# Four widths for each expert's matmuls, chosen on TensorE by the expert's token count

## The chip, the cores and the metric

The program runs on one core of one Trainium2 chip. The metric is device time in microseconds of one execution; before the change it is 400.27 us, the median of three runs (399.86 to 400.37). Engines are named as in the profile: PE is TensorE's matmul, PEld its weight load, PEldq its sequencer, DVE is VectorE, ACT ScalarE, POOL GpSimd, SP SyncE.

## What is computed

A retention layer (a decaying linear attention) is followed by a mixture of experts with one expert for each token:

```python
# q, k, v: (4, 8, 768, 64); x below has N = 3072 rows of D = 512
state = gamma * state + outer(k[t], v[t]);  y[t] = scale * q[t] @ state
...
logits = x @ w_gate                       # E = 8 experts
expert_idx = argmax(logits, axis=1);  gate_w = softmax(logits)[expert_idx]
for e in range(E):
    xe = x[expert_idx == e]
    h = maximum(xe @ w1[e], 0.0)          # 512 -> 1024
    out[expert_idx == e] = gate_w * (h @ w2[e])   # 1024 -> 512
```

How many tokens an expert gets is known only when the gate has been computed.

## The kernel before

The first 126 us compute the retention in chunks of 128 positions, the gate, and a scatter of the rows of x to one region of DRAM for each expert. Expert 0 is taken in two halves of up to 224 tokens: the first beside the last attention work, the second as step `e == 0` of `moe_main`. The other seven experts are sorted on the chip by their counts, the largest first, and take steps `e` = 1 to 7. Step `e` has a fixed room of `CAPS[e]` tokens (452, 424, 412, 400, 392, 376, 360), and its matmuls always work on all of it, however many tokens came. Tokens beyond the room would be left to `moe_rest`, behind a branch at the end (L646).

`moe_main` writes its order out by hand (`manual_schedule`). In a step, PE does eight *first-layer groups* (`f` = 0 to 7, L850): twelve matmuls each, three products of split operands (high by high, low weights by high, high weights by low) over four slices of D, into a PSUM tile `ph` of 128 features by `cap` tokens. ACT makes `hh` from `ph` (a ReLU, L855) and DVE `hl` (the rest that rounding leaves, L856). Then come four *second-layer groups* (`k` = 0 to 3, L878) of 24 matmuls each into `py`, 128 by `cap` again; DVE turns `py` into rows (L797). In steps 0 and 7 the second layer is done the other way round, tokens on the output's partitions and 512 columns wide (L876); there `cap` sets only how many partitions are used. `ph` is a ring of three PSUM tiles: group `f` can start when `hl` of group `f - 3` is done.

Around these groups the list `jobs` places other work behind the group where it stands: the loads of the next expert's weights (SP, L129), their split in high and low parts (ACT L137, DVE L138), the next expert's rows (`prep_x`), and the scatter of the last expert's results (POOL, L659).

Of the kernel before, what the change touches and what calls it, by code (L numbers as in the profile page):

```python
# [9 lines left out]
F32 = mybir.dt.float32  # L10
F32R = mybir.dt.float32r
BF16 = mybir.dt.bfloat16
I32 = mybir.dt.int32
AF = mybir.ActivationFunctionType
ALU = mybir.AluOpType
AX = mybir.AxisListType

B, H, S, D = 4, 8, 768, 64
E, DM, F = 8, 512, 1024
N = B * S  # L20
P = 128
# [5 lines left out]
NTOK = N // P  # L27
CAPS = [224, 452, 424, 412, 400, 392, 376, 360]
EARLY = 224
CMAX = max(CAPS)  # L30
CMAX32 = -(-CMAX // 32) * 32
E1 = E - 1
E9 = E + 1
KD = DM // P
KF = F // P
# [4 lines left out]
JMAX = -(-CMAX // 32)  # L40
# [17 lines left out]
_n = 0  # L58
for _name, _w in (("causal", 128), ("cv", 6 * H), ("ratio", 6 * (H // 2)), ("ident", 128), ("iota", 8),
                  ("desc", 16), ("tok", NTOK), ("blk", 24), ("ebase", E9),  # L60
                  ("rev", E1), ("eid", E1), ("caps", E1), ("row", 4), ("gate", 4 * E), ("slot", JMAX), ("place", 4)):
    OFF[_name] = (_n, _n + _w)
    _n += _w
NCONST = _n
# [3 lines left out]
def _constants():  # L68
    p = np.arange(P)
    c = np.zeros((P, NCONST), np.float64)  # L70

    def put(name, v):
        a, b = OFF[name]
        c[:, a:b] = v

    gamma = 1.0 - 2.0 ** (-5.0 - np.arange(H, dtype=np.float64))
    put("ident", np.eye(P))
    put("causal", (p[None, :] >= p[:, None]).astype(np.float64))
    put("iota", np.broadcast_to(np.arange(8)[None, :], (P, 8)))
    pos = (np.arange(6)[None, :] * C + p[:, None] + 1).astype(np.float64)  # L80
    put("cv", (gamma[None, None, :] ** (-pos[:, :, None])).reshape(P, 6 * H))
    order = np.concatenate([np.arange(E), np.arange(1, E), [0]])
    put("desc", np.broadcast_to(E - order[None, :], (P, 2 * E)))
    put("ebase", np.broadcast_to(N * np.array([E9, *range(1, E9)])[None, :], (P, E9)))
    put("rev", np.broadcast_to(E - 1 - np.arange(1, E)[None, :], (P, E1)))
    put("eid", np.broadcast_to(np.arange(1, E)[None, :], (P, E1)))
    put("caps", np.broadcast_to(np.array(CAPS[1:])[None, :], (P, E1)))
    put("row", np.broadcast_to(np.arange(4)[None, :], (P, 4)))
    put("slot", 32 * np.arange(JMAX)[None, :] + p[:, None] % 32)
    put("place", P * np.arange(4)[None, :] + p[:, None])  # L90
    put("blk", np.broadcast_to(P * np.arange(NJ, dtype=np.float64)[None, :], (P, NJ)))
    put("tok", np.arange(NTOK)[None, :] * P + p[:, None])
    pair = gamma.reshape(NP, 2).T
    put("ratio", np.repeat(pair[:, None, :] ** (C * np.arange(CPB))[None, :, None], D, axis=0).reshape(P, CPB * NP))
    turned = gamma.reshape(2, 2, 2).transpose(1, 2, 0).reshape(2, NP)
    g = np.zeros((2, DM + P), np.float64)
    g[:, 0:DM] = (turned[:, :, None] ** (np.arange(C) + 1.0)[None, None, :] / np.sqrt(np.float64(D))).reshape(2, DM)
    g[:, DM:] = np.repeat(np.eye(2), D, axis=1)
    return c.astype(np.float32), g.astype(np.float32)
# [3 lines left out]
def retention_moe(ctx, tc, qkv, wts, cst, gdec, out):  # L103
    nc = tc.nc
    pool = lambda name, bufs, **kw: ctx.enter_context(tc.tile_pool(name=name, bufs=bufs, **kw))
    PS = bass.MemoryType.PSUM
# [3 lines left out]
    k_ = lambda name: cs[:, OFF[name][0]:OFF[name][1]]  # L110
# [31 lines left out]
    wparts = {}  # L142
    expert_at, end_at = {}, {}

    gate = pool("gate", 1)
    xgs = gate.tile([P, 2, JMAX, W], F32, name="xgs")
# [8 lines left out]
    limit = gate.tile([P, E1, 1], F32, name="limit")  # L155
    beyond = gate.tile([P, E1, JMAX], I32, name="beyond")
# [2 lines left out]
    eid7, end7 = [gate.tile([P, E1], I32, name=n) for n in ("eid7", "end7")]  # L159
    top = gate.tile([P, 1], I32, name="top")  # L160
    run = gate.tile([P, E9], BF16, name="run")
    sel, se = [gate.tile([P, E1, E1], F32, name=n) for n in ("sel", "se")]
    us = gate.tile([P, P], BF16, name="us")

# [26 lines left out]
    with ExitStack() as actx:  # L191
        apool = lambda name, bufs, **kw: actx.enter_context(tc.tile_pool(name=name, bufs=bufs, **kw))
        gsm = apool("gsm", 1)
# [235 lines left out]
        for r in range(2):  # L429
            nc.vector.tensor_tensor(  # L430
                out=M[:, r], in0=causal.unsqueeze(1).broadcast_to([P, NP, C]), op=ALU.mult,
# [25 lines left out]
        for k in range(NCH // 2):  # L457
            a, b = 2 * k, 2 * k + 1
# [145 lines left out]
        nc.vector.tensor_tensor(out=se, in0=sel, in1=s7(cnt[:, 1:E]), op=ALU.mult)  # L604
        nc.vector.tensor_reduce(out=limit, in_=se, axis=AX.X, op=ALU.add)
        nc.vector.tensor_tensor(out=limit, in0=limit, in1=k_("caps").unsqueeze(2), op=ALU.min)
        far = gsm.tile([P, E1, JMAX], F32, name="far")
        nc.vector.tensor_tensor(out=far, in0=k_("slot").unsqueeze(1).broadcast_to([P, E1, JMAX]),
                                in1=limit.broadcast_to([P, E1, JMAX]), op=ALU.is_ge)
# [6 lines left out]
        xhl1 = new_xhl()  # L616
# [22 lines left out]
    def clear_behind(e, zero):  # L639
        nc.sync.dma_start(out=x_rows[bass.ds(end_at[e], ZROWS), :], in_=zero)  # L640

    natural = {0: (sidx8, meta8)}
    moe_main(tc, wparts, fetch, split, xhl1, xgs, clear_behind, load_x, load_meta, token_index, regions, beyond, limit, natural,
             overflow, out)
    most = nc.values_load(top[0:1, 0:1], min_val=0, max_val=N)
    with tc.If(most > 0):  # L646
# [83 lines left out]


@with_exitstack
def moe_main(ctx, tc, wparts, fetch, split, xhl1, xgs, clear_behind, load_x, load_meta, token_index, regions, beyond, limit, natural,
             overflow, out):
    nc = tc.nc
    pool = lambda name, bufs, **kw: ctx.enter_context(tc.tile_pool(name=name, bufs=bufs, reuse_waits="tile", **kw))
# [2 lines left out]
    hp = pool("hp", 1)  # L739
    yp = pool("yp", 2)  # L740
    tb = pool("tb", 1)
    ps_h = pool("ps_h", 3, space=PS)
    ps_y = pool("ps_y", 1, space=PS)

    widths = [[min(P, c - a) for a in range(0, c, P)] for c in CAPS]
    blocks = [-(-c // 32) for c in CAPS]
    xs = {0: (xhl1[:, 0], xhl1[:, 1])}
    pys = [ps_y.tile([P, DM], F32, name=f"py{i}") for i in range(2)]
    nc.vector.memset(pys[1][widths[0][1]:, CAPS[1]:], 0.0)
    out_slices = out.rearrange("n (q m) -> (n q) m", q=4)  # L750
    sidx = tb.tile([P, E1, JMAX], I32, name="sidx")
    gw = tb.tile([P, E1, JMAX, 1], F32, name="gw")
# [3 lines left out]
    zero = tb.tile([ZROWS, 4 * W], F32, name="zero")  # L756
    nc.gpsimd.memset(zero, 0.0)
    Zs = {}

    def fetch_x(e):  # L760
        clear_behind(e, zero)
# [45 lines left out]
    with tc.manual_schedule():  # L807
        for e in range(E):
# [11 lines left out]
                job(3, overflow)  # L820
            if e:
                job(2, index, e)
            if more and e:
                job(0, fetch_x, e + 1)
            if e > 0:
# [17 lines left out]
                    job(6, fetch, e + 1, 2)  # L843
            for f in range(KF):
                fo = (f % 4) * P
                ph = ps_h.tile([P, CMAX], F32, name="ph")
                n = 0
                for a, x in ((0, xh), (1, xh), (0, xl)):
                    for kd in range(KD):
                        nc.tensor.matmul(out=ph[:, :cap], lhsT=wparts[e, f // 4][a][:, kd, fo:fo + P],  # L850
                                         rhs=x[:, kd, :cap], start=(n == 0), stop=(n == 3 * KD - 1))
                        n += 1
                hh = hp.tile([P, CMAX], F32R, name="hh", tag="hh", bufs=9)
                hl = hp.tile([P, CMAX], F32R, name="hl", tag="hl", bufs=9)
                nc.scalar.activation(out=hh[:, :cap], in_=ph[:, :cap], func=AF.Relu)  # L855
                nc.vector.scalar_tensor_tensor(out=hl[:, :cap], in0=ph[:, :cap], scalar=0.0,  # L856
                                               in1=hh[:, :cap].bitcast(F32), op0=ALU.max, op1=ALU.subtract)
                hs.append((hh, hl))
                for fn, a in jobs[f]:
                    fn(*a)  # L860
            for k in range(steps):
                for j in range(nxt * k // steps, nxt * (k + 1) // steps) if e else range(nxt * (k == 0)):
                    prep_x(e + 1, j, nc.gpsimd if not e and j < 3 else nc.vector)
                if not e and k == 0:
                    for i, eng in halves:
                        split(1, 2, i, eng)
                py = pys[k % 2]
                n = 0
                for f in range(KF):
                    whi, wlo = wparts[e, 2 + f // 4]  # L870
                    hh, hl = hs[f]
                    for a, x in ((whi, hh), (wlo, hh), (whi, hl)):
                        se = dict(start=(n == 0), stop=(n == 3 * KF - 1))
                        if e in natural:
                            w = widths[e][k]
                            nc.tensor.matmul(out=py[:w, :], lhsT=x[:, k * P:k * P + w], rhs=a[:, f % 4, :], **se)  # L876
                        else:
                            nc.tensor.matmul(out=py[:, :cap], lhsT=a[:, f % 4, k * P:(k + 1) * P],  # L878
                                             rhs=x[:, :cap], **se)
                        n += 1  # L880
                if e in natural:
                    put_rows(e, py, k)
                else:
                    turn(e, py, k)
                if more and k < 2:
                    for i, eng in halves:
                        if e and i == k:
                            split(e + 1, 2, i, eng)
                if more and e and k == 0:
                    fetch(e + 1, 3)  # L890
                for fn, a in jobs[KF + k]:
                    fn(*a)
# [141 lines left out]
```

## Time and profile before

| | |
|---|---|
| median of the runs | 400.27 us |
| the profiled execution | 402.97 us |
| its span in the trace | 401.2 us |
| instructions in the trace | 8335 |
| PE busy, share of the span | 390.0 us, 97% |
| DVE, ACT, POOL busy | 245.7, 153.6, 164.4 us |
| last matmul starts at | 394.85 us of the span |

The profiled execution is one run under the hardware profiler; the 1.77 us between its time and its span lie outside of the trace, and the median run is 2.70 us shorter than it. Times inside of the trace are counted from the start of the span. In a group's row, the number behind x is how many instructions it holds; the time of one matmul in such a row is a modelled length, longer than the distance to the next matmul's start, since matmuls overlap. Here the distance is what counts.

### The profile page before, as it was taken

Reading aid. Unit: us, or ns where it says so; the run is one execution under the profiler, and the core shown is the slowest. Engines: PE = TensorE matmul, PEld = TensorE weight load, DVE = VectorE, ACT = ScalarE, POOL = GpSimd, SP = SyncE. Lnnn points to the kernel's source line nnn. Section 1 sums busy time; section 2 is a strip of 40 time slices with the busy share of each in tenths; the row PEclk is TensorE's granted clock in tenths of the full one; section 3 lists DMA queues with packets and bytes.
Section 4 is the critical chain, followed back from the end, with each engine's and each line's share of the span. In section 5 each row is a group of like instructions: output and inputs, shape, how many; then the busy total and the mean of one; then the engine's idle time right before and its main releaser. Section 6 shows DMA issues by size and latency. Waiting matters only on the chain.

```text
span 401.2 us, 8335 instructions
## 1 busy us (share of the span) xinstructions
PE 390.0 (97%) x3277; PEld 358.8 (89%) x3277; DVE 245.7 (61%) x470; ACT 153.6 (38%) x308; POOL 164.4 (41%) x153
## 2 busy tenths in 40 slices
PE   8999999998999999999999999999999999999994
PEld 4788888887987979999999999999999999999972
DVE  4448657777584756662866387467738657675320
ACT  2336345553631635431542345144324515523100
POOL 0324537866641050000385067118506822840642
PEclk9999999999899999999999999999999999999998
DMA  7998899995259596274358246825744672530111
GB/s 282 418 355 328 320 396 396 362 405 174 109 167 244 185 221 228 105 192 127 124 152 237 100 141 244 214 69 200 215 133 139 249 212 107 164 123 2 46 54 48
DMA packets 29645, 80.11 MB, mean 200 GB/s; under 512 B 4521, under 2 KB 18349, under 8 KB 23076
## 3 DMA queue, kind: packets, MB, share of 16 engines
q1 hardware_dynamic: 24596, 66.79, 50.7%
q0 software_dynamic: 5008, 12.77, 8.5%
q8 instruction: 26, 0.43, 0.4%
q14 instruction: 15, 0.12, 0.1%
HBM read 64.99 MB, written 15.08 MB: 200 GB/s over the span
## 4 chain that ended last, share of the span: by engine, by line
PE 89%; DMA 6%; issue 2%; SPq 1%; POOL 1%; DVE 1%; ACT 0%; POOLq 0%
PE ph L850 33%; PE py L878 27%; PE py L876 6%; PE Y L282 4%; PE sp L241 4%; DMA qkv_t<-qkv 3%; PE ph L701 3%; PE py L718 3%; DMA raw<-w 3%; PE xp L297 3%; PE Y L271 2%; PE U L255 2%; PE L L313 1%; PE lp L323 1%; POOL out L659 1%
## 5 line engine op out<-in xcount | busy, mean ns | idle before, releaser
L659 POOL DMA_INDIRECT out<-Z,sidx x80 | 93.1, 1164 | 143.9 <-DVE Z L802 104.3
L138 DVE TENSOR_TENSOR wlo<-raw,whi 128x1024 fp32r<-128x1024 f32 (+1 forms) x66 | 76.8, 1168 | 11.7 <-ACT whi L137 9.8
L855 ACT ACTIVATE hh<-ph 128x224 fp32r<-128x224 f32 (+7 forms) x64 | 31.2, 488 | 100.7 <-PE ph L850 97.3
L137 ACT CAST whi<-raw 128x1024 fp32r<-128x1024 f32 (+1 forms) x72 | 67.3, 951 | 2.2 <-DMA raw<-w 2.2
L878 PE MATMUL py<-hh,whi 128*128 128x452 f32 (+5 forms) x192 | 67.0, 349 | 0.0
L878 PE MATMUL py<-hl,whi 128*128 128x452 f32 (+5 forms) x192 | 66.9, 348 | 0.0
L878 PE MATMUL py<-hh,wlo 128*128 128x452 f32 (+5 forms) x192 | 66.9, 348 | 0.0
L856 DVE SCALAR_TENSOR_TENSOR hl<-ph,hh 128x224 fp32r<-128x224 f32 (+7 forms) x64 | 35.3, 552 | 40.2 <-ACT hh L855 36.3
L850 PE MATMUL ph<-xl,whi 128*128 128x452 f32 (+6 forms) x224 | 50.2, 346 | 0.0
L850 PE MATMUL ph<-xh,whi 128*128 128x452 f32 (+6 forms) x224 | 50.1, 345 | 0.0
L850 PE MATMUL ph<-xh,wlo 128*128 128x452 f32 (+6 forms) x224 | 50.0, 345 | 0.0
L850 PEld LDWEIGHTS ph<-xh,whi 128*128 128x128 f32 x224 | 40.7, 188 | 0.8
L850 PEld LDWEIGHTS ph<-xl,whi 128*128 128x128 f32 x224 | 40.8, 188 | 0.7
L850 PEld LDWEIGHTS ph<-xh,wlo 128*128 128x128 f32 x224 | 40.7, 188 | 0.7
L678 ACT CAST xh<-xt 128x512 fp32r<-128x512 f32 (+7 forms) x26 | 14.4, 555 | 59.7 <-DVE xt L669 57.1
L878 PEld LDWEIGHTS py<-hl,whi 128*128 128x128 f32 x192 | 36.1, 188 | 0.8
L878 PEld LDWEIGHTS py<-hh,whi 128*128 128x128 f32 x192 | 36.1, 188 | 0.7
L878 PEld LDWEIGHTS py<-hh,wlo 128*128 128x128 f32 x192 | 36.1, 188 | 0.7
L230 POOL TENSOR_TENSOR vs<-qkv_t,cs 128x512 f32<-128x512 f32 x19 | 19.7, 1038 | 37.9 <-DMA qkv_t<-qkv 29.1
L244 DVE TENSOR_TENSOR Sb<-sp,xgs 128x512 f32<-128x512 f32 x48 | 29.9, 683 | 4.7 <-PE sp L241 4.7
L797 DVE STREAM_TRANSPOSE Z<-py 128x416 f32<-128x416 f32 (+3 forms) x24 | 15.1, 627 | 27.3 <-PE py L878 25.0
L659 POOL DMA_INDIRECT xs_dram<-xn,KEY x24 | 25.9, 1079 | 8.1 <-issue 5.3
(138 smaller groups left out, 517.8 us busy)
## 6 DMA issues: line engine op xcount, KB each, us to landing
raw<-w SPq DMA_DIRECT2D x32, 1024.0 KB
qkv_t<-qkv SPq DMA_DIRECT2D x19, 1024.0 KB
qkv_t<-qkv SPq DMA_DIRECT2D x4, 768.0 KB
xgs<-xs_dram SPq DMA_DIRECT2D x12, 211.2 KB
xgs<-xs_dram SPq DMA_DIRECT2D x8, 195.0 KB
out<-Z,sidx POOLq DMA_INDIRECT x80
xs_dram<-zero SPq DMA_DIRECT2D x6, 195.0 KB
qkv_t<-qkv SPq DMA_DIRECT2D x2, 512.0 KB
```

The costliest lines, as they stand in the source:

```text
L137: nc.scalar.copy(out=hi[:, h], in_=raw[:, h])
L138: engine.tensor_tensor(out=lo[:, h], in0=raw[:, h], in1=hi[:, h].bitcast(F32), op=ALU.subtract)
L230: engine.tensor_tensor(out=vs, in0=qs[g][:, 2].rearrange("a (h d) -> a h d", d=D), in1=cv[:, c, :].unsqueeze(2).broadcast_to([P, H, D]), o ...
L241: nc.tensor.matmul(out=sps[r][:, p, :], lhsT=kt[half[r], p, :], rhs=q[half[r], p, :], start=True, stop=True)
L244: nc.vector.tensor_tensor(out=Sb[:, r], in0=sps[r], in1=M[:, r], op=ALU.mult)
L282: nc.tensor.matmul(out=Y[half[o], r, m * C:(m + 1) * C], lhsT=vp[:, p, half[r]], rhs=Sb[:, r, p, :], start=False, stop=True, skip_group_ch ...
L659: sc = tc.nc.gpsimd.indirect_dma_start(out=out, out_offset=bass.IndirectOffsetOnAxis(ap=index, axis=0), in_=rows, in_offset=None, bounds_c ...
L850: nc.tensor.matmul(out=ph[:, :cap], lhsT=wparts[e, f // 4][a][:, kd, fo:fo + P], rhs=x[:, kd, :cap], start=(n == 0), stop=(n == 3 * KD - 1))
L855: nc.scalar.activation(out=hh[:, :cap], in_=ph[:, :cap], func=AF.Relu)
L856: nc.vector.scalar_tensor_tensor(out=hl[:, :cap], in0=ph[:, :cap], scalar=0.0, in1=hh[:, :cap].bitcast(F32), op0=ALU.max, op1=ALU.subtract)
L876: nc.tensor.matmul(out=py[:w, :], lhsT=x[:, k * P:k * P + w], rhs=a[:, f % 4, :], **se)
L878: nc.tensor.matmul(out=py[:, :cap], lhsT=a[:, f % 4, k * P:(k + 1) * P], rhs=x[:, :cap], **se)
```

## The change

Each group of matmuls of steps 1 to 7 (both layers; in step 7 only the first) stands four times in PE's program, at `cap`, `cap - s`, `cap - 2s` and `cap - 3s` columns with `s = STEPS[e]` (10 in step 1, otherwise 8). DVE computes `spare`, a number from 0 to 3 for each of the seven experts: how many of the three narrower widths still hold the expert's tokens. PE loads the number of the next step into a register behind group `f == 4` and branches by it ahead of every group: two compare-and-branch instructions lead to one of four arms, and a jump leads from an arm's end to the code behind the four. ACT and DVE go on reading `cap` columns. So that the columns a narrow arm leaves out hold defined numbers, the ring `ph` becomes three fixed tiles, the columns behind 224 are cleared by DVE in step 0, and the clearing of `py1` begins 30 columns earlier.

```diff
+STEPS = [0, 10, 8, 8, 8, 8, 8, 8]
...
+    fewer = np.array(CAPS[1:])[None, :] - np.arange(1, 4)[:, None] * np.array(STEPS[1:])[None, :]
+    put("fewer", np.broadcast_to(fewer.reshape(1, 3 * E1), (P, 3 * E1)))
...
+    spare = gate.tile([P, E1], I32, name="spare")
...
         nc.vector.tensor_tensor(out=limit, in0=limit, in1=k_("caps").unsqueeze(2), op=ALU.min)
+        fits = gsm.tile([P, 3, E1], F32, name="fits")
+        nc.vector.tensor_tensor(out=fits, in0=limit.rearrange("p e o -> p o e").broadcast_to([P, 3, E1]),
+                                in1=k_("fewer").rearrange("p (s e) -> p s e", s=3), op=ALU.is_le)
+        with nc.allow_low_precision(reason="a sum of three comparisons"):
+            nc.vector.tensor_reduce(out=spare, in_=fits.rearrange("p s e -> p e s"), axis=AX.X, op=ALU.add)
...
-    ps_h = pool("ps_h", 3, space=PS)
+    ps_h = pool("ps_h", 1, space=PS)
...
+    phs = [ps_h.tile([P, CMAX], F32, name=f"ph{i}") for i in range(3)]
     pys = [ps_y.tile([P, DM], F32, name=f"py{i}") for i in range(2)]
-    nc.vector.memset(pys[1][widths[0][1]:, CAPS[1]:], 0.0)
+    nc.vector.memset(pys[1][widths[0][1]:, CAPS[1] - 3 * STEPS[1]:], 0.0)
...
+    def count_columns(e):
+        fewer[e] = nc.tensor.value_load(spare[0:1, e - 1:e], min_val=0, max_val=3)
+
+    def by_count(e, products):
+
+        if e == 0:
+            return products(CAPS[0])
+        with tc.If(fewer[e] < 2) as few:
+            with tc.If(fewer[e] < 1) as none:
+                products(CAPS[e])
+            with none.Else():
+                products(CAPS[e] - STEPS[e])
+        with few.Else():
+            with tc.If(fewer[e] < 3) as two:
+                products(CAPS[e] - 2 * STEPS[e])
+            with two.Else():
+                products(CAPS[e] - 3 * STEPS[e])
...
+            if more:
+                job(4, count_columns, e + 1)
...
-                ph = ps_h.tile([P, CMAX], F32, name="ph")
-                n = 0
-                for a, x in ((0, xh), (1, xh), (0, xl)):
-                    for kd in range(KD):
-                        nc.tensor.matmul(out=ph[:, :cap], lhsT=wparts[e, f // 4][a][:, kd, fo:fo + P],
-                                         rhs=x[:, kd, :cap], start=(n == 0), stop=(n == 3 * KD - 1))
-                        n += 1
+                ph = phs[(KF * e + f) % 3]
+
+                def first_layer(w):
...
+                            nc.tensor.matmul(out=ph[:, :w], lhsT=wparts[e, f // 4][a][:, kd, fo:fo + P],
+                                             rhs=x[:, kd, :w], start=(n == 0), stop=(n == 3 * KD - 1))
...
+                by_count(e, first_layer)
+                if e == 0 and f < 3:
+                    nc.vector.memset(ph[:, cap:], 0.0)
...
+                def second_layer(cols):
...
+                                nc.tensor.matmul(out=py[:, :cols], lhsT=a[:, f % 4, k * P:(k + 1) * P],
+                                                 rhs=x[:, :cols], **se)
...
+                if e in natural:
+                    second_layer(cap)
+                else:
+                    by_count(e, second_layer)
```

On PE, the start of step 2 reads as follows before the change; `xh` and `xl` are the parts of x, `whi` and `wlo` those of the weights, and a row with x4 stands for four matmuls:

```order
L850 MATMUL ph<-xh,whi 128x424 [waits Activation_49]
L850 MATMUL ph<-xh,whi 128x424 x3
L850 MATMUL ph<-xh,wlo 128x424 x4
L850 MATMUL ph<-xl,whi 128x424 [waits DVE_49]
L850 MATMUL ph<-xl,whi 128x424 x3
L850 MATMUL ph<-xh,whi 128x424 x4
```

In the changed program the second first-layer group of step 2 (the last row above begins it) stands at this place, with its tests and its first two arms:

```order
L779 COMPARE_AND_BRANCH
L780 COMPARE_AND_BRANCH
L884 MATMUL ph_2146<-xh,whi 128x424 x4
L884 MATMUL ph_2146<-xh,wlo 128x424 x4
L884 MATMUL ph_2146<-xl,whi 128x424 x4
L780 UNCONDITIONAL_BRANCH
L884 MATMUL ph_2146<-xh,whi 128x416 x4
L884 MATMUL ph_2146<-xh,wlo 128x416 x4
L884 MATMUL ph_2146<-xl,whi 128x416 x4
L780 UNCONDITIONAL_BRANCH
L785 COMPARE_AND_BRANCH
```

Behind these come the arms of 408 and 400 columns with a jump each; the waits of a group (for ACT, for DVE) stand inside of every arm, on the same matmuls as before, and the tests stand ahead of them.

On DVE, the place where the experts' limits are computed reads so before the change, while PE still works on the first half of expert 0:

```order
L605 TENSOR_REDUCE limit<-se 128x7 [waits DVE_49]
L606 TENSOR_TENSOR limit<-limit,cs 128x7 [waits DVE_49]
L608 TENSOR_TENSOR far<-cs,limit 128x105 [waits DVE_49]
L610 TENSOR_SCALAR beyond<-far 128x105 [waits DVE_49]
L709 TENSOR_TENSOR hl_1616<-rx_1614,hh_1615 128x224 [waits Activation_49] x2
```

and so in the changed program, where two instructions stand ahead of `far`:

```order
L611 TENSOR_TENSOR limit<-limit,cs 128x7 [waits DVE_49]
L613 TENSOR_TENSOR fits<-limit,cs 128x21 [waits DVE_49]
L616 TENSOR_REDUCE spare<-fits 128x7 [waits DVE_49]
L618 TENSOR_TENSOR far<-cs,limit 128x105
L620 TENSOR_SCALAR beyond<-far 128x105 [waits DVE_49]
```

The clearing of the three `ph` tiles stands on DVE in step 0 ahead of the `hl` of the same group, and waits for PE alone:

```order
L890 MEMSET ph_2144 128x228 [waits PE_49]
L894 SCALAR_TENSOR_TENSOR hl<-ph_2144,hh 128x224 [waits Activation_49]
L890 MEMSET ph_2145 128x228 [waits PE_49]
L894 SCALAR_TENSOR_TENSOR hl<-ph_2145,hh 128x224 [waits Activation_49]
L890 MEMSET ph_2146 128x228 [waits PE_49]
```

Before, three `hl` follow each other there with nothing between them. DVE, ACT, POOL and SP each also get an unconditional branch in their programs for each of the 80 branched groups, to the place that follows on that engine anyway.

## Rows read from the trace of the kernel before

**Rows 1.** The page: busy time of PE, and its granted clock in 40 slices.
```profile
PE 390.0 (97%) x3277; PEld 358.8 (89%) x3277; DVE 245.7 (61%) x470; ACT 153.6 (38%) x308; POOL 164.4 (41%) x153
...
PEclk9999999999899999999999999999999999999998
```
**Rows 2.** Waits of PE over the span, the last row: total, times, longest (us).
```profile
PE ph L850 <- DVE far L185: 0.9, 1, 0.9
```
**Rows 3.** Busy time by step, 1 to 7 (step 7 its first layer); header first.
```profile
core 0: us, PE busy (x) PEld busy (x) DVE busy (x) ACT busy (x) POOL busy (x), PEclk, DMA share, GB/s
147.94:187.26 39.32, 39.32 (x194) 36.08 (x193) 23.04 (x37) 14.10 (x20) 1.86 (x2) 1.00 0.62 181
187.26:224.38 37.12, 37.12 (x194) 36.07 (x192) 23.65 (x35) 13.87 (x20) 17.90 (x15) 1.00 0.54 165
224.38:260.44 36.06, 36.06 (x194) 35.93 (x192) 23.33 (x35) 13.75 (x20) 15.94 (x14) 1.00 0.54 165
260.44:295.39 34.95, 34.95 (x194) 34.95 (x192) 23.02 (x35) 13.64 (x20) 15.00 (x13) 1.00 0.58 178
295.39:329.72 34.33, 34.33 (x193) 34.33 (x193) 22.47 (x33) 13.34 (x19) 16.74 (x13) 1.00 0.56 170
329.72:362.66 32.94, 32.94 (x194) 32.94 (x194) 21.86 (x33) 13.27 (x19) 15.84 (x13) 1.00 0.36 126
362.66:378.35 15.69, 15.69 (x97) 15.69 (x97) 7.83 (x19) 4.70 (x8) 6.54 (x7) 1.00 0.08 26
```
**Rows 4.** Timeline of PE at borders of steps: start, length, instruction.
```profile
147.94 0.37 PE L850 MATMUL ph<-xh,whi 128*128 128x452 f32 x1
...
187.25 0.36 PE L850 MATMUL ph<-xh,whi 128*128 128x424 f32 x1
...
378.35 0.39 PE L876 MATMUL py<-whi,hh 128*128 128x512 f32 x1
```
**Rows 5.** Busy time in an attention stretch, and in step 0's first layer.
```profile
59.23:63.60 4.37, 4.37 (x104) 3.99 (x104) 3.58 (x13) 2.06 (x7) 2.21 (x3) 1.00 1.03 395
126.02:136.80 10.78, 10.78 (x96) 10.78 (x97) 5.98 (x13) 6.09 (x11) 0.93 (x1) 1.00 0.75 199
```
**Rows 6.** Lines 646 and 645: lengths min/median/max (ns), first and last start (us).
```profile
L646 SPq EVENT_SEMAPHORE  x5: 17/17/17, 349.7 to 350.1; - x5
...
L646 POOLq EVENT_SEMAPHORE  x2: 17/17/17, 397.1 to 397.2; - x2
L646 SPq COMPARE_BRANCH  x1: 53/53/53, 349.5 to 349.5; - x1
L646 PEldq COMPARE_BRANCH  x1: 358/358/358, 391.5 to 391.5; - x1
...
L646 POOLq COMPARE_BRANCH  x1: 45/45/45, 396.9 to 396.9; - x1
...
L645 PEldq TENSOR_LOAD <-top x1: 487/487/487, 390.9 to 390.9; - x1
```
**Rows 7.** Timeline of PE beside the load and branch, and its last matmul.
```profile
390.91 0.40 PE L876 MATMUL py<-whi,hh 128*104 128x512 f32 x1
...
394.85 0.40 PE L876 MATMUL py<-whi,hl 128*104 128x512 f32 x1
```
**Rows 8.** The page's DMA queues: packets, MB, share of 16 engines' span.
```profile
q8 instruction: 26, 0.43, 0.4%
```
**Rows 9.** Timelines of DVE and PE in step 7: `hl` of `f = 2`, start of `f = 5`.
```profile
369.83 0.53 DVE L856 SCALAR_TENSOR_TENSOR hl<-ph,hh 128x360 fp32r<-128x360 f32 x1
...
372.47 0.49 PE L850 MATMUL ph<-xh,whi 128*128 128x360 f32 x2
```
**Rows 10.** Timeline of DVE: the limits, the wait behind them, a memset, step 0's first `hl`.
```profile
116.40 0.17 DVE L606 TENSOR_TENSOR limit<-limit,cs 128x7 f32<-128x7 f32 x1
...
119.58 0.75 DVE L722 TENSOR_SCALAR xn<-py,meta 128x512 f32<-128x512 f32 x1 [1.45 <-PE py L718]
...
1.46 0.49 DVE L422 MEMSET xgs<- 96x520 f32 x1
128.01 0.39 DVE L856 SCALAR_TENSOR_TENSOR hl<-ph,hh 128x224 fp32r<-128x224 f32 x1 [1.67 <-ACT hh L855]
```

More of the change, by code (lines that the diff above doesn't have):

```diff
@@ L60 @@
                   ("desc", 16), ("tok", NTOK), ("blk", 24), ("ebase", E9),
-                  ("rev", E1), ("eid", E1), ("caps", E1), ("row", 4), ("gate", 4 * E), ("slot", JMAX), ("place", 4)):
+                  ("rev", E1), ("eid", E1), ("caps", E1), ("fewer", 3 * E1), ("row", 4), ("gate", 4 * E), ("slot", JMAX), ("place", 4)):
     OFF[_name] = (_n, _n + _w)
@@ L642, in retention_moe @@
     natural = {0: (sidx8, meta8)}
-    moe_main(tc, wparts, fetch, split, xhl1, xgs, clear_behind, load_x, load_meta, token_index, regions, beyond, limit, natural,
+    moe_main(tc, wparts, fetch, split, xhl1, xgs, clear_behind, load_x, load_meta, token_index, regions, beyond, limit, spare, natural,
              overflow, out)
@@ L732, in moe_main @@
 @with_exitstack
-def moe_main(ctx, tc, wparts, fetch, split, xhl1, xgs, clear_behind, load_x, load_meta, token_index, regions, beyond, limit, natural,
+def moe_main(ctx, tc, wparts, fetch, split, xhl1, xgs, clear_behind, load_x, load_meta, token_index, regions, beyond, limit, spare, natural,
              overflow, out):
@@ L758, in moe_main @@
     Zs = {}
+    fewer = {}
+    def count_columns(e):
[13 more added lines that the diff above has]
+                products(CAPS[e] - 3 * STEPS[e])
     def fetch_x(e):
@@ L845, in moe_main @@
                 fo = (f % 4) * P
-                ph = ps_h.tile([P, CMAX], F32, name="ph")
-                n = 0
-                for a, x in ((0, xh), (1, xh), (0, xl)):
-                    for kd in range(KD):
-                        nc.tensor.matmul(out=ph[:, :cap], lhsT=wparts[e, f // 4][a][:, kd, fo:fo + P],
-                                         rhs=x[:, kd, :cap], start=(n == 0), stop=(n == 3 * KD - 1))
-                        n += 1
+                ph = phs[(KF * e + f) % 3]
+                def first_layer(w):
+                    n = 0
+                    for a, x in ((0, xh), (1, xh), (0, xl)):
+                        for kd in range(KD):
+                            nc.tensor.matmul(out=ph[:, :w], lhsT=wparts[e, f // 4][a][:, kd, fo:fo + P],
+                                             rhs=x[:, kd, :w], start=(n == 0), stop=(n == 3 * KD - 1))
+                            n += 1
+                by_count(e, first_layer)
+                if e == 0 and f < 3:
+                    nc.vector.memset(ph[:, cap:], 0.0)
                 hh = hp.tile([P, CMAX], F32R, name="hh", tag="hh", bufs=9)
@@ L867, in moe_main @@
                 py = pys[k % 2]
[L868 to L880, printed above, removed]
+                def second_layer(cols):
+                    n = 0
+                    for f in range(KF):
+                        whi, wlo = wparts[e, 2 + f // 4]
+                        hh, hl = hs[f]
+                        for a, x in ((whi, hh), (wlo, hh), (whi, hl)):
+                            se = dict(start=(n == 0), stop=(n == 3 * KF - 1))
+                            if e in natural:
+                                w = widths[e][k]
+                                nc.tensor.matmul(out=py[:w, :], lhsT=x[:, k * P:k * P + w], rhs=a[:, f % 4, :], **se)
+                            else:
+                                nc.tensor.matmul(out=py[:, :cols], lhsT=a[:, f % 4, k * P:(k + 1) * P],
+                                                 rhs=x[:, :cols], **se)
+                            n += 1
+                if e in natural:
+                    second_layer(cap)
+                else:
+                    by_count(e, second_layer)
                 if e in natural:
```

## The prediction

> **What bounds the kernel now.** [...] PE's waits are short and early; the last is 0.9 us, at the start of step 0 [rows 2], and from 126 us to the last matmul PE waits for nobody. Then I cut the expert steps apart [rows 3], at the borders that the timeline shows where the width of the matmul changes [rows 4]. Each of steps 1 to 6 is 192 matmuls, step 7's first layer 96, and PE is busy for the whole of each stretch. Divided, one matmul takes 204.8 ns at 452 columns (39.32 us by 192), 193.3 at 424, 187.8 at 412, 182.0 at 400, 178.8 at 392, 171.6 at 376 and 163.4 at 360 (15.69 by 96). Time goes with the width: 41.4 ns for 92 columns, 0.45 ns a column.
>
> A floor under the matmul would end this. The weight load's row is as long as the matmul's step from 400 columns down (34.95 of 34.95), which looks like one; but the modelled lengths overlap, and 96 matmuls of 224 columns took 10.78 us, 112 ns each, with loads of the same shape [rows 5]. The floor is thus at or under 112 ns, and 352 columns, the least width here, are far above.
>
> **What the narrower arms remove.** Which arm runs follows from the inputs alone. Evaluating the reference's gate on its inputs gives 417, 413, 404, 387, 387, 358 and 347 tokens in the order of the steps, all within the rooms. By the test (the count fits in the width) the arms are the fourth, second, second, second, first, third and second: 422, 416, 404, 392, 392, 360 and 352 columns. With the times of one matmul above, interpolated between the two nearest widths:
> - step 1: from 452 to 422, 204.8 to 192.4 ns, 192 times: 2.38 us
> - step 2: 424 to 416, 3.7 ns: 0.70; step 3: 412 to 404, 3.9 ns: 0.74; step 4: 400 to 392, 3.2 ns: 0.61
> - step 5: nothing
> - step 6: 376 to 360, 8.2 ns: 1.57
> - step 7, first layer: 360 to 352, extrapolated at the last slope of 0.51 ns a column, 4.1 ns, 96 times: 0.39
>
> Together 6.4 us. [...] No other engine holds PE back from it: DVE has 23.65 us of work in a step of 37.12, ACT and POOL less, and DMA is at 0.62 or under [rows 3].
>
> **What the branches add.** 80 groups (eight and four in steps 1 to 6, eight in step 7) get two tests and at most one jump each: up to 240 instructions of PE's sequencer. The trace has one test on PE, behind the last matmul in the program. It took 358 ns, the register load ahead of it 487 [rows 6]. Neither drained PE: the load started at 390.9 us, beside the matmul of 390.91, while the last matmul that stands ahead of it in the program started at 394.85, 17 steps of 0.23 us later [rows 7]. So the sequencer was 17 matmuls, 3.9 us, ahead of the array, and whatever it does within its lead costs nothing. The price hangs on whether its work per group fits.
>
> A group's work: 104 matmuls and 104 loads went out in 4.37 us [rows 5], so an instruction needs at most 21 ns, and a first-layer group of 24 half a microsecond. A test that jumps and reaches its target takes 0.2 us on SP (349.5 to 349.7) and on POOL (396.9 to 397.1); PE's length alone is 358 ns and the time to its target isn't seen, so 0.5 us is my upper bound (358 ns and the 0.15 us that SP and POOL need behind the test). Three of these make 0.6 to 1.5 us, so a first-layer group costs the sequencer 1.1 to 2.0 us. The array needs 12 matmuls, 1.91 us (352 columns) to 2.31 us (422). I take the lower half, since SP's and POOL's tests took 53 and 45 ns, but even the upper bound is 0.1 us over in step 7 alone, 0.8 us for eight groups, and the lead covers that. In the second layer 48 instructions and the tests make 1.6 to 2.5 us against 3.8 to 4.6 of array, which refills the lead.
>
> The lead itself is also bounded by the three `ph` tiles: a group can't be issued before `hl` of three groups earlier. I looked this distance up for every group of steps 1 to 7; the shortest is in step 7, where `hl` ends at 370.36 and the group starts at 372.47, 2.1 us [rows 9]. The tests stand ahead of that wait in the program, so they run while PE's sequencer would wait anyway. Cost of the branches: nothing to 0.8 us; I take 0.4 us for places where the lead is short.
>
> **Instructions to load.** PE's program is loaded while it runs: 26 packets, 0.43 MB, so 16.5 KB each, for 6,554 matmuls and loads, one for about 252 instructions [rows 8]. The four arms make each first-layer group about 103 instructions long and each second-layer group about 199, 10,500 in place of 2,500, so some 32 packets more. A packet took 0.4% of 16 engines' 401.2 us by 26, 1.0 us. The program position then moves through 252 instructions in about 5 us of array time, where it took 24; the next part is there in 1 us if it is asked for at the entry of the present one. No jump here is longer than 150 instructions, so none passes over a whole part. Cost: nothing if so; the other case is the first rival. SP's and POOL's tests, which jump too, reached their target within 0.2 us, too short for a 1.0 us packet [rows 6, 8].
>
> [...]
>
> **The small parts.** Seven register loads on PE, 0.49 us each with some register work, stand behind `f == 4` and lie in the lead, as the one in the trace did. `fits` and `spare` are two DVE instructions of some 0.2 us (a 128x7 one took 0.17); behind them DVE has 1.45 us of waiting for PE [rows 10], which takes them up; without it they would cost 0.4 us once. Three clearings of 228 columns, about 0.22 us each by the 0.49 us of 520 elements, wait for PE alone, while the `hl` behind them waits for ACT; DVE was idle for 1.67 us ahead of the first [rows 10]. Uncovered they would cost 0.7 us. The branches of the other engines, 80 each, cost at most 0.2 us each by SP's row, between instructions that wait for PE: nothing. The 21 more columns of constants are loaded early, under the attention.
>
> **The sum.** 6.4 us less, 0.4 us more: 6.0. On the profiled execution's 402.97 us that is 397.0. The median of the runs is 2.70 us under it; the change keeps that, so 400.27 - 6.0 = 394.3 us.
>
> **Rivals.**
> - *Every taken jump reloads PE's instructions* (slower). In four of the five kinds of path a group takes two jumps (an odd test, and the leap over the other arms), in step 5 one. Each would hold the sequencer for the 1.0 us of a packet: a first-layer group then costs 0.5 + 0.6 + 2.0 = 3.1 us against 1.9 to 2.3. Over by 0.8, 0.8, 0.9, 0.95, 0, 1.1 and 1.2 us in steps 1 to 7, eight times each: 46 us, less six leads of about 2.5 us: 31, less the 6.4: some 425 us. For: no row shows PE behind a jump, and PE's test took seven times as long as SP's. Against: SP and POOL. It decides from about 2.1 us of control for a first-layer group on: 2.14 us of mean array time, less the 0.5 us of issue, plus an eighth of a 2.5 us lead and a 56th of 6.4 us.
> - *The lead is partly lost* (a smaller gain): a test that waits until the queue has shrunk, or instruction packets that come late at some of the 41 borders of parts. If each of the 80 groups leaves PE idle for 40 ns, 3.2 us are lost: 397.5 us. At 80 ns nothing is left of the gain, 400.3.
> - *A floor at the width*: if step 7's 163 ns were the least that a matmul takes, 0.39 us would be lost, 394.7; it moves little and [rows 5] speak against it.
>
> **How the numbers follow.** Forecast 0.64, partial loss 0.13, nothing left 0.04, reload or another slow branch 0.19. The likeliest time is 394.3 us, its own range 393.3 (6.6 us saved, nothing paid, and 0.4 us of scatter between runs) to 396. Downwards little is left out under 393.0; upwards I reach over the partial loss to 403, which leaves out most of the slow rival, about 0.16. A change of 0.2% (0.8 us) is about what a measurement here can tell from none. Faster 0.76, same 0.05, slower 0.19.
>
> **What would show it.** Right: steps 1 to 7 each as long as 192 (or 96) matmuls at the new width, 36.9, 36.4, 35.3, 34.3, 34.3, 31.4 and 15.3 us, PE busy throughout; some 58 instruction packets on q8 in place of 26; the tests of a group start a microsecond or more ahead of the group's first matmul. Wrong: idle time of PE at the start of groups with nothing of DVE or ACT that ends it ("issue"), most of all in first-layer groups, or steps longer than before in all but their number of columns; tests that start only when the array has run dry.

## The result, and the profile after

The changed kernel took 393.92 us (median of five runs, 393.75 to 395.3), the kernel before on the same chip 400.19 us (399.86 to 400.37): a ratio of 0.9849, 95% interval 0.9826 to 0.9873. 394.3 us had been forecast. Of the twelve runs of the changed kernel on record (these five and the seven of e4 below) one, of 402.62 us, is left out of the ratios; the others lie between 393.75 and 397.80 us.

The profiled execution after took 393.84 us. Of its page, the lines that answer to [rows 1] and [rows 8]:

```profile
span 392.1 us, 8599 instructions
...
PE 381.4 (97%) x3277; PEld 354.1 (90%) x3277; DVE 248.5 (63%) x475; ACT 153.9 (39%) x308; POOL 164.2 (42%) x153
...
PEclk9999999999999999999999999999999999999999
...
q8 instruction: 58, 0.95, 1.0%
```

PE still fills its span, on as many matmuls as before, at a granted clock of nine tenths of full speed or more in every slice (mean 0.998); 58 instruction packets came in place of 26.

The busy time by step, cut where the first matmul of each step starts, in the columns of [rows 3]:

```profile
145.09:181.89 36.80, 36.80 (x194) 36.10 (x193) 22.84 (x37) 14.10 (x20) 1.87 (x2) 1.00 0.66 196
181.89:218.39 36.50, 36.50 (x194) 35.88 (x193) 23.59 (x35) 13.87 (x20) 17.38 (x15) 1.00 0.53 153
218.39:253.56 35.17, 35.17 (x194) 35.16 (x193) 23.27 (x35) 13.82 (x20) 16.93 (x14) 1.00 0.63 192
253.56:287.86 34.30, 34.30 (x194) 34.29 (x193) 22.91 (x35) 13.65 (x20) 15.90 (x13) 1.00 0.58 178
287.86:322.10 34.24, 34.24 (x193) 34.24 (x193) 22.39 (x33) 13.46 (x19) 16.66 (x13) 1.00 0.52 155
322.10:353.74 31.64, 31.64 (x193) 31.64 (x193) 21.75 (x33) 13.29 (x19) 15.04 (x13) 1.00 0.46 158
353.74:369.22 15.48, 15.48 (x98) 15.48 (x97) 8.55 (x21) 5.18 (x9) 6.37 (x7) 1.00 0.09 29
```

Read down the first length: against [rows 3] the steps are shorter by 2.52, 0.62, 0.89, 0.65, 0.09, 1.30 and 0.21 us. That is 6.28 us, all of the 6.27 us between the medians. That this execution enters step 1 2.85 us earlier (145.09 for 147.94) isn't counted as a gain: in nine of the kernels below (e1 to e3, e5, e6, e9 to e12), whose program is nearly the same up to there, that entry lies between 145.6 and 148.4 us, and in the trace of e4, the same kernel, at 150.27.

The tests have rows now. L779 is the first test of a group, L780 the second with the jumps of the first two arms, L785 the same for the last two; columns as in [rows 6]:

```profile
L779 PEldq COMPARE_BRANCH  x80: 65/70/1232, 141.0 to 364.8; - x80
...
L780 PEldq COMPARE_BRANCH  x112: 65/208/2637, 178.6 to 366.4; - x112
...
L785 PEldq COMPARE_BRANCH  x36: 65/176/872, 141.3 to 350.8; - x36
```

A test that falls through takes 65 to 70 ns, one that jumps 208, the jump at an arm's end 176: some 0.45 us for a group, under the 0.6 us that the sum had as its lower bound. The longest lengths in the rows are the warning: single ones took up to 2.64 us. The longest is a jump at the end of an arm of step 3, and the timeline shows what it cost PE:

```profile
L780 PEldq COMPARE_BRANCH  x1: 2637/2637/2637, 219.5 to 219.5; - x1
```
```profile
221.30 0.89 PE L884 MATMUL ph<-xh,wlo 128*128 128x404 f32 x4
222.04 0.90 PE L884 MATMUL ph<-xl,whi 128*128 128x404 f32 x4
222.77 0.71 PE L884 MATMUL ph<-xh,whi 128*128 128x404 f32 x3
```

While the sequencer stood from 219.49 to 222.13, the array went on with what it had been given, and the next group started on time at 222.77; its first test ran at 222.19, 0.58 us ahead. That was the shortest distance of the 80 groups (median 2.83 us). What held it was the loading of instructions: the one packet on q8 in 219.55 to 222.80 went out at 219.62 and took 1.02 us, and the jump was through 1.5 us after it had landed. It is no single case: all ten tests and jumps over 0.6 us in this trace end 1.2 to 1.5 us after a packet has landed, and so do 112 of the 113 in e3 and e11 below.

### The profile page after: what moved, and what is told of

Its sections match the earlier page's. It is cut to its first block, busy times and chain, and to the rows that moved or that the text cites. A ratio compares the mean times of both kernels' runs of the same rounds, so it can differ in the third digit from the quotient of the medians.

```text
span 392.1 us, 8599 instructions
## 1 busy us (share of the span) xinstructions
PE 381.4 (97%) x3277; PEld 354.1 (90%) x3277; DVE 248.5 (63%) x475; ACT 153.9 (39%) x308; POOL 164.2 (42%) x153
## 4 chain that ended last, share of the span: by engine, by line
PE 91%; DMA 3%; DVE 2%; issue 2%; SPq 1%; POOL 1%; POOLq 0%
PE ph L884 33%; PE py L918 27%; PE py L916 6%; PE sp L246 5%; PE Y L287 5%; PE xp L302 3%; DMA qkv_t<-qkv 3%; PE py L728 3%; PE ph L711 3%; PE Y L276 2%; PE U L260 2%; PE L L318 2%; PE lp L328 1%; POOL out L669 1%; SPq L225 0%
## 5 line engine op out<-in xcount | busy, mean ns | idle before, releaser
L142 DVE TENSOR_TENSOR wlo<-raw,whi 128x1024 fp32r<-128x1024 f32 (+1 forms) x66 | 78.9, 1200 | 11.2 <-ACT whi L141 11.0
L918 PE MATMUL py<-hh,whi 128*128 128x392 f32 (+4 forms) x192 | 66.0, 344 | 0.0
L918 PE MATMUL py<-hl,whi 128*128 128x392 f32 (+4 forms) x192 | 65.9, 343 | 0.0
L918 PE MATMUL py<-hh,wlo 128*128 128x392 f32 (+4 forms) x192 | 65.9, 343 | 0.0
L884 PE MATMUL ph<-xh,wlo 128*128 128x392 f32 (+5 forms) x224 | 49.1, 341 | 0.0
L884 PE MATMUL ph<-xh,whi 128*128 128x392 f32 (+5 forms) x224 | 48.9, 340 | 0.0
L884 PE MATMUL ph<-xl,whi 128*128 128x392 f32 (+5 forms) x224 | 48.8, 339 | 0.0
```

What stands on the lines that cost most here:

```text
L142: engine.tensor_tensor(out=lo[:, h], in0=raw[:, h], in1=hi[:, h].bitcast(F32), op=ALU.subtract)
L884: nc.tensor.matmul(out=ph[:, :w], lhsT=wparts[e, f // 4][a][:, kd, fo:fo + P], rhs=x[:, kd, :w], start=(n == 0), stop=(n == 3 * KD - 1))
L918: nc.tensor.matmul(out=py[:, :cols], lhsT=a[:, f % 4, k * P:(k + 1) * P], rhs=x[:, :cols], **se)
```

## The experiments

The kernels ran in three groups of four, each group on one chip beside the kernel before, which took 402.05 us beside e1 to e4, 401.46 beside e5 to e8 and 401.66 beside e9 to e12; so ratios compare best. Behind a ratio stands its 95% interval. "The steps" is the time from the first matmul of step 1 to the end of step 7's first layer, in the profiled execution: 230.41 us before, 224.13 after.

**e1, branches without a narrower width.** All four arms have the old width (the fourth runs).
```diff
-STEPS = [0, 10, 8, 8, 8, 8, 8, 8]
+STEPS = [0, 0, 0, 0, 0, 0, 0, 0]
```


> All four arms of each group have the old width (all steps 0, so the fourth arm runs); the tests, jumps, the longer program and DVE's extra work stay. Theory A (the gain is the columns alone, the branches hide in the sequencer's lead): as before the change, 400.2 us, at most 0.4 more. Rival B (branches leave PE idle and eat part of the gain): 401 to 403. Rival C (the gain comes from elsewhere, since the profiled execution after the change also has a first part that is 2.8 us shorter): 394 to 398.

Measured: 407.57 us (405.98 to 410.51), ratio 1.0143 (1.0109 to 1.0176): slower by 5.5 us, more than any theory had. The trace is of the shortest of the six runs, 3.9 us over the kernel before. Its steps take 234.46 us, 4.05 more than before, and 3.9 us of that is step 3 (39.99 for 36.06). The waits of PE, timeline and windows there:

```profile
PE py L918 <- DVE Z L827: 2.2, 1, 2.2
```
```profile
250.20 0.35 PE L918 MATMUL py<-hl,whi 128*128 128x412 f32 x1
252.79 0.71 PE L918 MATMUL py<-hh,whi 128*128 128x412 f32 x1 [2.23 <-DVE Z L827]
253.30 0.55 PE L918 MATMUL py<-hh,wlo 128*128 128x412 f32 x1
...
252.12 0.62 DVE L827 STREAM_TRANSPOSE Z<-py 128x416 f32<-128x416 f32 x1 [3.97 <-DMA out<-Z,sidx]
```
```profile
248.00:250.00 2.00, 2.00 (x12) 1.99 (x11) 0.15 (x1) 0.38 (x1) 1.39 (x3) 1.00 0.90 332
250.00:252.00 2.00, 0.55 (x3) 0.21 (x2) 0.00 (x0) 0.00 (x0) 0.82 (x1) 1.00 0.80 294
252.00:254.00 2.00, 1.21 (x4) 1.18 (x5) 1.88 (x3) 0.00 (x0) 0.00 (x0) 0.66 0.22 33
254.00:256.00 2.00, 2.00 (x7) 1.94 (x6) 1.31 (x3) 1.50 (x2) 0.00 (x0) 0.50 1.09 220
```

PE waits at `k = 2` for the tile that DVE turns after `k = 0`. DVE turns it 6 us after PE's last matmul of `k = 0` (246.0), where it is 0.04 us in 21 of the 24 turns of the kernel before and 0.50 at most. So PE's next matmul starts 2.4 us late. Then the granted clock is 0.50 for some 3 us behind the gap: 343 ns for a matmul that takes 188, which costs another 1.6 us. So the loss in this trace is a wait of 2.4 us and the 0.50 clock behind it, at one place, and no test stood still there; the other six steps are as long as in e5, which has no branches.

**e2, the narrower widths without branches.** The widths of the arms that run are written in; the tests, jumps and register loads go.
```diff
+FIXED = [224, 422, 416, 404, 392, 392, 360, 352]
...
+        return products(FIXED[e])
```


> The seven widths that the counts of this input select (422, 416, 404, 392, 392, 360, 352) are written into the program, with no tests, jumps or register loads; all else is as in the changed kernel. It holds for this input alone. Theory A: 0.1 to 0.4 us under the changed kernel, so 393.5 to 393.8. Rival B: 1 to 3 us under it, 391 to 393.

Measured: 396.62 us, ratio 0.9861 (0.9834 to 0.9889); the steps 223.96 us, no wait of PE in them, 26 instruction packets. Its step 2, in the columns of [rows 3]:

```profile
184.02:220.34 36.32, 36.32 (x194) 35.97 (x193) 23.60 (x35) 13.88 (x20) 17.38 (x15) 1.00 0.58 169
```

So in the changed kernel's first trace the branches cost 0.17 us of the steps (all of it in step 2, 36.50 for 36.32). The times show no cost (0.9861 here, 0.9854 for the changed kernel beside it in e4), but each is known to about 1.1 us only, so it's the steps that tell this.

**e3, eight arms.** Steps of 6 and 4 columns; the tests are a binary tree.
```diff
+STEPS = [0, 6, 4, 4, 4, 4, 4, 4]
...
+        def among(lo, n):
+            if n == 1:
+                return products(CAPS[e] - lo * STEPS[e])
+            with tc.If(fewer[e] < lo + n // 2) as low:
+                among(lo, n // 2)
+            with low.Else():
+                among(lo + n // 2, n // 2)
+
+        among(0, 8)
```


> Eight arms in place of four, with half the step (6 columns in step 1, 4 in the others): widths 422, 416, 404, 388, 388, 360, 348, 2688 columns fewer than the changed kernel, some 1.2 us. The program of steps 1 to 7 grows from 41 to about 84 parts of 252 instructions. Theory A with one part loaded ahead: in the changed kernel's trace the longest tests end 1.2 to 1.5 us after an instruction packet's end, and the next packet starts 0.7 us after them, so a part takes 0.7 + 1.0 + 1.4 = 3.1 us from its request until it can be used; 84 of them are 260 us where the matmuls need 223, so loading becomes the bound: 420 to 440 us. Theory D (the lead covers whatever is added, loading runs far ahead): 392.7.

Measured: 490.8 us, ratio 1.2193 (1.2138 to 1.2247); the steps 318.22 us. Its packets by the page, and the first two waits of PE:

```profile
q8 instruction: 99, 1.62, 1.4%
```
```profile
PE ph L884 <- issue: 20.8, 23, 4.3
PE py L918 <- issue: 18.5, 11, 3.7
```

PE's waits in the steps come to 63.8 us: 39.3 for its own sequencer ("issue"), 35.6 of them at the first matmul of a group, and 24.5 put down to DVE and ACT. 64 tests and jumps took over 1.5 us, 175 us in all. In the steps 81 packets went out, none sooner than 3.00 us after the one before. PE's mean granted clock over the span is 0.952 (0.991 before), so a part of the loss stands in the clock. Loading became the bound, as theory A had it, but its 420 to 440 us were 50 us too few: 84 parts of 3.1 us make 260 us, and the steps took 318.

**e4, the changed kernel again.** No edit; a second measurement beside e1 to e3.

> The changed kernel as it is, beside the others on this chip: 393.9 us by every theory. It is the base for e2, whose difference is a few tenths.

Measured: 396.16 us (395.18 to 402.62), ratio 0.9854 (0.9827 to 0.988), as in the first measurement and as e2. The trace is of the run of 402.62 us. It enters step 1 5.2 us later than the first trace, and its steps take 227.74 us, 3.6 us more, all of them in step 2 (40.10 for 36.50). A wait of PE in step 2, the last matmul of `k = 0` with its turn on DVE, and the step:

```profile
PE py L918 <- issue: 2.4, 5, 0.9
```
```profile
209.60 0.35 PE L918 MATMUL py<-hl,whi 128*128 128x416 f32 x1
...
217.28 0.65 DVE L827 STREAM_TRANSPOSE Z<-py 128x448 f32<-128x448 f32 x1 [4.60 <-remote]
```
```profile
187.07:227.17 40.10, 37.60 (x194) 35.82 (x194) 23.56 (x35) 13.88 (x20) 15.70 (x15) 1.00 0.48 142
```

The turn is late by 7.3 us, as it was in e1, and PE's five waits stand inside of one group, between 212 and 217 us, where there is no test and no jump. So one program with the same arms lost 0.2 us of its steps in one execution and 3.8 us in another (against e2's). What made the difference, the two traces don't show.

**e5, the rest of the change at the old widths.** As e2, with the old widths, one arm and no branch.
```diff
+FIXED = [224, 452, 424, 412, 400, 392, 376, 360]
```


> All that the change adds except the branches (three fixed tiles, the clearings, the two DVE instructions), at the old widths, one arm for each group. Theory A, the 5.7 us that the branches at old widths cost come from the branches: this kernel takes the time of the kernel before, within 1.0 us. Theory B, they come from the other added parts: 4 to 7 us above the kernel before.

Measured: 401.7 us, ratio 1.0 (0.9983 to 1.0018), the steps 230.49 us. The fixed tiles, the clearings and the DVE instructions cost nothing that can be told (the interval is 0.7 us to either side); e1's 5.5 us come with the branches.

**e6, the first arm.** As e1, but the register gets 0.
```diff
-    put("fewer", np.broadcast_to(fewer.reshape(1, 3 * E1), (P, 3 * E1)))
+    put("fewer", np.full((P, 3 * E1), -1.0))
```


> Branches at the old widths as before, but the number that PE loads is 0 for every expert, so the first arm runs: two tests that don't jump, and one jump over three arms at the end, in place of two jumping tests and no jump at the end. If the 5.7 us are the price of every branch (0.07 us for each of 80 groups): again 4 to 7 us above the kernel before. If they hang on where jumps come to stand against the borders of the loaded parts: another number, most likely within 1.5 us of the kernel before, with no late turn in step 3.

Measured: 402.44 us, ratio 1.0023 (1.0004 to 1.0041), the steps 230.94 us: 0.4 us lost in step 4, none in step 3.

**e7, e1 half a part later.**
```diff
-WARM = 12
+WARM = 76
...
-            nc.tensor.matmul(out=warm, lhsT=ones, rhs=ones.unsqueeze(1).broadcast_to([P, 4, P]), start=True, stop=True)
+            nc.tensor.matmul(out=warm[:, 0:80], lhsT=ones, rhs=ones[:, 0:80], start=True, stop=True)
```


> Branches at the old widths, fourth arm as in the first run, but the twelve warming matmuls of 512 columns at the start are 76 of 80 columns: as much array time, 128 more instructions, so everything behind stands half a part later in the loaded parts. If the stall in step 3 hangs on where jumps stand against the borders of parts: it is gone or at another place, and the time is 0 to 3 us above the kernel before. If not: 5 to 6.5 us above it, with the late turn in step 3 again.

Measured: 404.34 us, ratio 1.0077 (1.0044 to 1.011), the steps 232.15 us. The late turn of step 3 is gone; 0.6 us are lost there and 1.0 us in step 6, where PE waits for its sequencer:

```profile
PE py L918 <- issue: 1.2, 2, 0.8
```

So the same branches with the same work lose 4.0, 0.5 or 1.7 us in the steps of these three traces. That the arm or the place has a part in it the ratios show too: e6's interval lies below those of e1 and e7. That these alone decide isn't shown, since there is one trace for each kernel, and e4's shows such a loss in one execution of a program and not in the other.

**e8, the changed kernel half a part later.** The edit of e7.

> The changed kernel with the same 128 instructions more at the start. If the place against the borders of parts matters little with the arms that run here: ratio 0.984 to 0.987, as without it. If it matters: up to 5 us more, ratio up to 0.998, with a late turn in some step's second layer.

Measured: 397.49 us, ratio 0.9892 (0.9863 to 0.992). The steps take 224.15 us, as without the shift. It enters step 1 at 148.64 us, later than all traces but e4's; whether the 64 added loads and matmuls at the start do that isn't settled, so of e7's ratio too only the 1.7 us in the steps are counted here.

**e9, steps fitted to these counts.** Widths 420, 414, 404, 388, 388, 358, 348.
```diff
-STEPS = [0, 10, 8, 8, 8, 8, 8, 8]
+STEPS = [0, 16, 10, 8, 6, 4, 6, 6]
```


> The changed kernel with STEPS = [0, 16, 10, 8, 6, 4, 6, 6], so that the arms for these counts are 420, 414, 404, 388, 388, 358 and 348 columns. By 0.45 ns a column it saves 1.4 us more than the changed kernel: 394.4 us where that took 395.8, ratio about 0.982. The jumps then lead to other arms (third, second, second, third, second, fourth, third), so if places against the borders of parts decide, it may lose up to 5 us of that: ratio up to 0.994.

Measured: 394.28 us (391.99 to 396.52), ratio 0.9815 (0.9783 to 0.9847); the steps 223.09 us, 1.0 us under the changed kernel's, one gap of 0.4 us in step 6 among them.

**e10, three arms.** The tree of e3 with three arms, 16 columns apart in step 1, 8 elsewhere: the widths of the change, 420 in step 1.
```diff
-STEPS = [0, 10, 8, 8, 8, 8, 8, 8]
+STEPS = [0, 16, 8, 8, 8, 8, 8, 8]
...
+        among(0, 3)
```


> Three arms in place of four, 16 columns apart in step 1 and 8 in the others: the same widths as in the changed kernel for these counts, but 420 in step 1 (0.2 us less). A quarter fewer instructions to load (some 47 packets of 16.4 KB). If loading costs the changed kernel nothing, ratio 0.984 to 0.986, PE without any gap in steps 1 to 7; if it costs something on the average run, 0.5 to 2 us less than that.

Measured: 394.18 us (394.07 to 395.33), ratio 0.983 (0.9814 to 0.9845), 47 packets:

```profile
q8 instruction: 47, 0.77, 0.8%
```

The steps take 223.84 us, e2's less the 0.13 us of two columns in step 1: no matmul of them is late.

**e11, six arms.** The tree with six arms, 6 and 4 columns apart.
```diff
+STEPS = [0, 6, 4, 4, 4, 4, 4, 4]
...
+        among(0, 6)
```


> Six arms, 6 columns apart in step 1 and 4 in the others: 0.9 us less matmul work than the changed kernel. If one part of 252 instructions needs 3.1 us from request to use, the some 64 parts of the steps need 198 us against 223 us of matmuls, so on average they are in time: 394 to 400 us if only the average counts. If parts that are jumped through quickly are what costs, PE waits in many groups: 405 to 440 us, between four arms and eight (490.8).

Measured: 428.28 us, ratio 1.0679 (1.0634 to 1.0724), the steps 258.77 us. Packets, and the first two waits of PE:

```profile
q8 instruction: 78, 1.28, 1.2%
```
```profile
PE py L918 <- issue: 14.1, 9, 3.2
PE ph L884 <- DVE hl L894: 5.2, 3, 2.2
```

61 packets in the steps at 3.1 us are 189 us, less than the matmuls' 223: on average they would be in time. They are not, so the average doesn't decide. 43 tests and jumps took over 0.6 us, the longest 6.08. A late turn stands in this trace too, 3.3 us in step 3.

**e12, two tiles for the first layer.**
```diff
-    phs = [ps_h.tile([P, CMAX], F32, name=f"ph{i}") for i in range(3)]
+    phs = [ps_h.tile([P, CMAX], F32, name=f"ph{i}") for i in range(2)]
```


> The changed kernel with a ring of two tiles in place of three for the first layer, so PE's sequencer can be at most about one group ahead there. If the tests are all that has to be hidden (0.6 us for a group): no more than 1 us above the changed kernel, ratio 0.984 to 0.988. If the lead also hides the loading of instructions: PE gaps at the start of first-layer groups and 3 to 10 us more, ratio 0.993 to 1.01.

Measured: 396.67 us, ratio 0.9899 (0.9872 to 0.9925). Inconclusive: the first tests still ran 2.69 us (median, least 1.09) ahead of their groups, so the edit didn't shorten the lead it was to shorten. The steps take 224.59 us, 0.5 us over the changed kernel's, and 0.8 us are lost in step 0, which has no branches.

## Why the prediction was right, and where it wasn't

- *What bounds the kernel, and the widths* (6.4 us saved): shown. PE is still busy for 381.4 of 392.1 us; the gain is 6.28 us, step by step within 0.3 us of the terms; e2 saves the same with no branch. A matmul of 352 columns takes 161 ns, so step 7 gained 0.21 us in place of 0.39; that isn't a floor, since 348 columns took 158 ns in e9. The 6.6 us that the forecast's range begins with no run shows; the runs showed 6.28 us in the steps, and 6.45 in e2's.
- *The tests lie in the lead*: shown by the steps (e2 against the changed kernel) and in the rows: 0.45 us for a group, inside a lead of 2.83 us in the median, and of over 1 us in 79 of the 80 groups.
- *The other parts cost nothing*: shown by e5, to 0.7 us.
- *0.4 us for places where the lead is short*: 0.17 us in the first trace. But the size is no property of the branches. The same 80 groups of branches lost between 0.5 and 4.0 us in the steps (e1, e6, e7), and 3.8 us in the other execution of the changed kernel that has a trace (e4). So the term stands for the usual run of this program with these counts only. A run with other counts takes other arms; e6 against e1 shows that this alone can move the median by 1.2%. That the term came out so small was in part luck: the forecast held, its certainty on this term wasn't earned.
- *Instructions to load*: the number of packets (58) was right, the argument on time wrong. It took the 1.0 us of a packet for the time from the request to use. A packet lands after 1.0 us, a held jump goes on 1.2 to 1.5 us after that, and the next packet goes out some 0.7 us later (the median behind the ten long ones is 0.74). So in every kernel with branches the shortest distance from one packet to the next is 3.0 to 3.1 us (3.00 with eight arms, 3.08 with six, 3.06 in the first trace with four and with three). With four arms a part lasts 5.5 us on average (224 us by 41 packets), and the lead takes up the rest.
- *The rival of a lead that is partly lost*, "instruction packets that come late at some of the 41 borders of parts": it had 13 in 100, and late packets are really there, though in the changed kernel's usual run the lead hides them. Against the sum of the same widths without branches the steps lose nothing with three arms, 0.2 us with four, 36 with six and 95 with eight (with six and eight, e9's shorter steps 4, 5 and 7 are set in). The likeliest reading is that a sequencer that jumps over five arms in six passes through some parts with only a microsecond or two of matmuls in them (estimated from the 12 matmuls of 161 to 192 ns in one arm of the first layer, 1.9 to 2.3 us) and stands at the next; which part that was isn't seen in the trace, so it is argued from e11 alone.
- *The rival in which every taken jump reloads*: refuted. 112 rows at L780 have a median of 208 ns, 36 at L785 176, where it had 1.0 us for each jump. (Its count is off: there are four kinds of path, three with two jumps and one with one. Its sum has the right number for each step.) Of all 228 rows of tests and jumps ten are over 0.6 us, and those ten end 1.2 to 1.5 us after a packet has landed.
- *From the profiled execution to the median*: the 2.70 us that were to stay between them are 0.08 after (393.84 and 393.92 us). Nothing hung on it, since the 6.0 us were taken off the median.

Open: e1's late turn. Its DVE had nothing left to do, the scatters that the turn also waits for had landed, and the trace's semaphore events have PE's count rise at 252.06 to 252.09 only, 6.4 us after the start of the matmul that raises it. Late turns stand only in traces of kernels with branches (e1, e3, e11, and e4, which is the changed kernel), but not in all of those (not in e6, e7 or the changed kernel's first trace). Late counts as such need no branches: in step 7 they stand in the kernel before (2.3 us), in e5 (2.3) and in e2 (3.9) as well, where PE waits for none of them. So whether branches cause the late turn isn't shown, and what delays the counts no run shows.

## What to carry to other kernels

Code that stands several times for the sake of a branch was paid here in instructions to load (packets of some 250, never closer than 3.0 us), not in tests (0.45 us for a group, inside of the lead). So count how long the array works on each such part, and leave each well above those 3.0 us; three arms were free here, four nearly in the usual run, six lost 36 us. Fewer or better placed widths did no worse than the change: three arms (0.983) and four fitted steps (0.9815, for this input's counts alone) stand beside its 0.985, with intervals that overlap, so neither is shown to be better. A branch that costs nothing in one build, or in one execution, is no evidence for the next: repeat the measurement with the program shifted or with another arm, and look at more than one trace.

## What was not expected of the hardware

- The 3.0 us between two instruction packets, with packets of 1.0 us, whatever the demand: 81 packets in the steps with eight arms and none closer than 3.00 us.
- PE went on for 2.6 us while its sequencer stood in one jump, without one late matmul (219.49 to 222.13 in the first trace).
- A gap of 2.4 us in PE's work (e1) was followed by some 3 us at a granted clock of 0.50, which cost another 1.6 us; matmuls of 412 columns took 343 ns in place of 188.
- PE's count of finished groups reached DVE 6 us late in e1 while PE went on with its matmuls at the usual distance, and 7 us late in one of the two executions of the changed kernel that left a trace (e4).
